# Moving a softmax scale from VectorE to ScalarE, four subtractions from TensorE to VectorE, and two places in the order

## The chip, the cores and the metric

One core of a Trainium2 chip runs the whole program. The metric is the device time of one execution in microseconds (us), the median of several runs. TensorE (PE) multiplies matrices, VectorE (DVE) and ScalarE (ACT) work elementwise, SyncE (SP) issues every DMA. Each engine works through its own queue in the written order and waits on semaphores.

## The reference

Eight batches of eight heads: x is 512 x 64 per head, state 32 x 64. A cross attention in both directions, then two feed-forward layers over the 4608 rows of 512 features that come out.

```python
scores = scale * np.matmul(x, state.transpose(0, 1, 3, 2))     # then softmax over the 32 states
xread = np.matmul(a, state)
scores2 = scale * np.matmul(state, x.transpose(0, 1, 3, 2))    # then softmax over the 512 rows
a2 /= a2.sum(-1, keepdims=True) + 1e-09
sread = np.matmul(a2, x)
attn_out = np.concatenate([xread, sread], axis=2)
h = x @ w_in;  r = np.maximum(h, 0.0);  g = s * (r * r) + b;  x = g @ w_out      # first layer
h = np.maximum(x @ w_in2, 0.0);  out = h * h @ w_out2                            # second layer
```

## The kernel before

Products are made in two fp32r parts (hi and lo): a tensor is copied to its hi part, and its lo part is the difference. A product is then three matmuls, hi by hi, hi by lo, lo by hi.

**The first layer** fills the span to about 620 us. Its rows are never formed for the reads of x: state times w_in is formed instead (the tensor S, one part per batch b and quarter q of the 2048 hidden features, in two halves r, so the tile S43 is batch 4's quarter 3, and S430 and S431 are its two PSUM tiles), and `mm1` multiplies S by the transposed attention weights aT. The list `order` says which block (j, f) of batch j and hidden feature block f is worked on in each step. A step is six matmuls of `mm1` into a tile h, three passes of ScalarE over it (`relu2`: Relu, Square, the copy to g's hi part), VectorE's `low` (g's lo part), and twelve matmuls of `mm2`, two steps later, into four accumulators acc. In blocks of the first two batches the raw weights are also converted on the way (`early`).

**Around the steps**, side jobs are put at fixed steps with `at_step(step, job, rank)`; within a step they run by rank. For batch b from 2 on, counted from its own base (base is 16 steps on from one batch to the next), step 5 makes the scores and S of quarter 0, steps 6 to 10 the softmax (`att_max`, `att_exp`, `att_sum`, `att_mul`), step 13 the transposed weights, and step 17 these, in this order: `att_sr` (rank 0: 32 calls that read x with the transposed weights, into the PSUM tile sr), `s_mm` of quarter 2 (rank 1: matmuls into two PSUM tiles, two copies on ScalarE to S's hi part), `att_scale` (rank 2: sr times the inverse of the softmax's sum s2, into srs), and `s_mm` of quarter 3 (rank 2.5). Ahead of these, in the same step, `mm2` closes the accumulators of batch b-1, and `evac` takes them out: two tiles by VectorE, two by ScalarE, each stored at once; the next `mm2` comes behind S of quarter 3.

**PSUM tiles** for all of these come from `pst`, which goes round four banks:

```python
    banks = itertools.cycle((psa, psb, psc, psc))
    def pst(name, pool=None):
        return (pool or next(banks)).tile([P, 512], F32, tag="ps", name=name)
```

A tile waits until the last reader of the tile that held its bank is done. At step 17 five tiles are taken in a row: sr, two for quarter 2, two for quarter 3.

**For batch 0**, S is made in pairs of blocks (`s_pair`), and `s_pair_lo`, one step later, makes the lo part: a matmul with minus the identity adds minus hi to the PSUM tile, and ScalarE copies the rest out.

**Lines** that the rows below name: L613 `mm1`, L643 `mm2`, L626 `low`, L350 `per_head` (the scores and S), L361 and L367 S's hi copies and lo subtractions, L560 `att_sr`, L579 and L581 the scale on ScalarE and on VectorE, L418 the matmul with minus the identity, L547 the copy of the transposed weights, L660 and L669 `evac`, L176 the last step of a conversion, L286 a job's hi copy.

**The table SUMS_AT** gives, for each of 16 jobs that prepare the second layer's weights, the steps of its 15 parts: two times (magnitude, clamp, bits), the sums, four hi copies on ScalarE, four lo subtractions on VectorE. A job's part e is stored one step after its lo subtraction. Its raw tiles and hi tiles come from one pool of four (`rawp`).

**The second layer** follows, from about 620 us to the end: a product of seven partial products per block, whose weights are loaded from DRAM.

Of the kernel before, what the change touches and what calls it, by code (L numbers as in the profile page):

```python
# [27 lines left out]
F32 = mybir.dt.float32  # L28
F32R = mybir.dt.float32r
U32 = mybir.dt.uint32  # L30
ACTF = mybir.ActivationFunctionType
ALU = mybir.AluOpType
# [16 lines left out]
VA = 4  # L49

CUTS = (0, 4, 10, NF)
# [37 lines left out]
def attn_mlp2(ctx: ExitStack, tc: tile.TileContext, xT, xn, st, w_in1, w_out1, w_in2, w_out2, s_in, b_in, out):  # L89
    nc = tc.nc  # L90
    scale = 1.0 / float(D) ** 0.5
# [8 lines left out]
    op = ctx.enter_context(tc.tile_pool(name="op", bufs=4))  # L100
# [11 lines left out]
    minus = const.tile([P, P], F32R, name="minus")  # L112
# [18 lines left out]
    def x8(shape, name, dt=F32R):  # L131
        return xp.tile(shape, dt, tag="x", name=name)
# [222 lines left out]
    def s_mm(b, q):  # L355

        t = S_t[b, q] = w8([P, 2, 2, 512], f"S{b}{q}")
        pts = [pst(f"S{b}{q}{r}") for r in range(2)]
        per_head(pts, sb_t[b], lambda rows, k: V1[q][rows, k, :])
        for r, pt in enumerate(pts):  # L360
            nc.scalar.activation(out=t[:, 0, r, :], in_=pt, func=ACTF.Copy)  # L361
            S_ps[b, q, r] = pt

    def s_rest(b, q):
        t = S_t[b, q]
        for r in range(2):
            nc.vector.tensor_tensor(  # L367
                out=t[:, 1, r, :], in0=S_ps.pop((b, q, r)), in1=t[:, 0, r, :].bitcast(F32), op=ALU.subtract
            )
# [44 lines left out]
    def s_pair_lo(f):  # L414
        q, fo = f // FQ, f % FQ * P
        t, cols = S_t[0, q], slice(fo, fo + 2 * P)
        for r, pt in enumerate(S_ps.pop(f)):
            nc.tensor.matmul(  # L418
                out=pt, lhsT=minus, rhs=t[:, 0, r, cols], start=False, stop=True, skip_group_check=True
            )  # L420
            nc.scalar.activation(out=t[:, 1, r, cols], in_=pt, func=ACTF.Copy)

    def s_lo(b, q, c):
        t, pt = S_t[b, q], S_ps.pop((b, q, c))
# [9 lines left out]
    def st_load(b):  # L434
        sb = sm.tile([P, 2, KD, NS], F32, tag="st", name=f"st{b}")
        nc.sync.dma_start(out=sb, in_=st[b])
        sb_t[b] = sb

    def att_load(b):
        t = x8([P, KD, S], f"xT{b}", F32)  # L440
        kk = KD // 2 if b < 2 else KD
        for k in range(0, KD, kk):
            nc.sync.dma_start(
                out=t[:, k : k + kk, :], in_=xT[b, k * P : (k + kk) * P].rearrange("(k p) s -> p k s", p=P)
            )
        xa[b] = [t, None]

    def att_load_n(b):
        n = x8([P, S // P, DM], f"xn{b}", F32)
        nc.sync.dma_start(out=n, in_=xn[b].rearrange("(t p) d -> p t d", p=P))  # L450
        xa[b][1] = n
# [39 lines left out]
    def att_exp(b, between=None):  # L491
        t1 = cur[b][1]
        m1 = an1.tile([P, 32, 1], F32, tag="m1", name="m1")
        nc.vector.tensor_reduce(out=m1[:, :, 0], in_=t1, axis=AX.X, op=ALU.max)
        if between:
            between()
        nc.vector.tensor_tensor(out=t1, in0=t1, in1=m1.to_broadcast([P, 32, 32]), op=ALU.subtract)
        nc.scalar.activation(out=t1, in_=t1, func=ACTF.Exp, scale=1.0 if b else scale)

    parts2 = {}  # L500

    def inverse(s, between=None):
        nc.vector.tensor_scalar(out=s, in0=s, scalar1=1e-9, scalar2=None, op0=ALU.add)
        if between:
            between()
        nc.vector.reciprocal(out=s, in_=s)
# [24 lines left out]
    def att_turn(b, c):  # L531
        turned[b, c] = att_an(b, c)
# [36 lines left out]
    def att_scale(b):  # L569
        srp = srp_t.pop(b)  # L570
        s2 = parts2.pop(b)
        if b > 1:
            inverse(s2)
        t = an1.tile([P, P], F32, tag="an", name="srs").rearrange("p (r d) -> p r d", r=2)
        srp_t[b] = t
        for r in range(2):
            src, by = srp[:, r * D : (r + 1) * D], s2[:, r : r + 1]
            if b < 2:
                nc.scalar.activation(out=t[:, r], in_=src, func=ACTF.Copy, scale=by)  # L579
            else:  # L580
                nc.vector.tensor_scalar(out=t[:, r], in0=src, scalar1=by, scalar2=None, op0=ALU.mult)  # L581

    def att_put(b):
        t = srp_t.pop(b)
        pt = pst(f"st{b}")[:, :P]
        nc.tensor.transpose(out=pt, in_=t.rearrange("p r d -> p (r d)"), identity=ident)
        dst, src = sraw[:, :, b * NS : (b + 1) * NS], pt.rearrange("p (k n) -> p k n", k=KD)
        nc.scalar.activation(out=dst, in_=src, func=ACTF.Copy)
# [547 lines left out]
    def at_step(i, fn, rank=5):  # L1136

        side.setdefault(i, []).append((rank, len(side.get(i, ())), fn))
# [5 lines left out]
    def step(j, f):  # L1144
        return place[j, 0] + f
# [4 lines left out]
    for b in range(1, B):  # L1150
        base = step(2, 0) + (b - 3) * NF if b > 1 else 0
        if b > 1:
            at_step(base + 1 + (b == 2), lambda b=b: st_load(b), 6)
            at_step(base + 1, lambda b=b: att_load(b), 6)
            at_step(base + 1, lambda b=b: att_load_n(b), 6)
            for fn, k, r in calm:
                at_step(base + k, lambda fn=fn, b=b: fn(b), r)
            for c in range(2):
                n = base + 11 + c
                at_step(n, lambda b=b, c=c: att_turn(b, c), 3)  # L1160
                at_step(n, lambda b=b, c=c: turned.pop((b, c))(), 6)
            at_step(base + (21 if b < B - 1 else 18), lambda b=b: att_put(b), -1)
            for q, (k, r) in enumerate(((5, 1), (13, 1), (17, 1), (17, 2.5))):
                at_step(base + k, lambda b=b, q=q: s_mm(b, q), r)
            at_step(base + 5 + (b == 2), lambda b=b: s_rest(b, 0), 0.2 if b == 2 else 9.8)
            at_step(base + 13, lambda b=b: s_rest(b, 1), 9.8)
            behind[base + 17] = lambda b=b: s_rest(b, 2)
            at_step(base + 18, lambda b=b: s_rest(b, 3), 0.2)
            continue
        for q, n in ((1, 12), (2, 16), (3, 23)):  # L1170
            at_step(n, lambda b=b, q=q: s_mm(b, q), 1)
            at_step(n + 1, lambda b=b, q=q: s_rest(b, q), 0.2)
# [70 lines left out]
    for f, i in zip(range(VA, NF, 2), (6, 8, 10, 15, 17, 18)):  # L1243
        at_step(i, lambda f=f: s_pair(f), 0.5)
        pre[i + 1] = [lambda f=f: s_pair_lo(f)]
# [40 lines left out]
    with tc.manual_schedule():  # L1286
# [33 lines left out]
        lo = [att_an(0, c) for c in range(2)]  # L1320
# [68 lines left out]
        lo = [att_an(1, c) for c in range(2)]  # L1389
# [14 lines left out]
        begin(4)  # L1404
        o1(3)["lo"]()
        att_scale(1)
        convert(4)
        bring(6)
# [73 lines left out]
```

## Time and profile before

| | us |
|---|---|
| median of 3 runs (1322.65 to 1323.81) | 1323.28 |
| the profiled execution's own time | 1323.02 |
| its span, first to last instruction | 1321.2 |
| TensorE busy in the span | 1304.6 (99%) |
| VectorE busy | 921.9 (70%) |
| ScalarE busy | 807.1 (61%) |

The busy times are from the head of the profile. Matmuls are pipelined and their ends are modelled, so a busy TensorE is not one without waits: a matmul's start is the safer mark. In the rows below L12 is line 12 of the kernel before; names are the program's tiles without their numbers. The granted clock is a share of TensorE's 2.4 GHz.

### The profile page before, as it was taken

Reading aid. Unit: us, or ns where it says so; the run is one execution under the profiler, and the core shown is the slowest. Engines: PE = TensorE matmul, PEld = TensorE weight load, DVE = VectorE, ACT = ScalarE, POOL = GpSimd, SP = SyncE. Lnnn points to the kernel's source line nnn. Section 1 sums busy time; section 2 is a strip of 40 time slices with the busy share of each in tenths; the row PEclk is TensorE's granted clock in tenths of the full one; section 3 lists DMA queues with packets and bytes.
Section 4 is the critical chain, followed back from the end, with each engine's and each line's share of the span. In section 5 each row is a group of like instructions: output and inputs, shape, how many; then the busy total and the mean of one; then the engine's idle time right before and its main releaser. Section 6 shows DMA issues by size and latency. Waiting matters only on the chain.

```text
span 1321.2 us, 21087 instructions
## 1 busy us (share of the span) xinstructions
PE 1304.6 (99%) x7434; PEld 1115.6 (84%) x7434; DVE 921.9 (70%) x1609; ACT 807.1 (61%) x1485; POOL 0.7 (0%) x7
## 2 busy tenths in 40 slices
PE   6999999999999999999999999999999999999998
PEld 4677777778787877788988888888899999999998
DVE  7988988766676767655556668656775776678665
ACT  5877657676666667665744565545555565565554
POOL 0000000000000000000000000000000000000000
PEclk8999999999999999999999999999999999999999
DMA  8367443453725254451465577665887798788775
GB/s 280 129 215 258 153 145 109 144 183 105 255 92 204 88 180 157 131 171 38 160 199 174 176 247 219 207 173 171 258 259 230 227 323 255 227 265 298 246 223 167
DMA packets 159560, 255.68 MB, mean 194 GB/s; under 512 B 14816, under 2 KB 67040, under 8 KB 159200
## 3 DMA queue, kind: packets, MB, share of 16 engines
q1 hardware_dynamic: 159456, 254.34, 60.2%
q8 instruction: 60, 0.98, 0.3%
q14 instruction: 44, 0.36, 0.1%
HBM read 202.90 MB, written 51.38 MB: 192 GB/s over the span
## 4 chain that ended last, share of the span: by engine, by line
PE 95%; DVE 3%; ACT 1%; DMA 0%; issue 0%; DVEq 0%
PE acc L643 27%; PE p L899 25%; PE m L875 25%; PE h L613 15%; PE S L350 2%; PE sr L560 1%; PE sc L350 1%; PE tp L546 0%; DMA i1r<-w_in 0%; DVE sraw L316 0%; DVE g L626 0%; DVE V L169 0%; DVE part L660 0%; DVE v L169 0%; DVE V L176 0%
## 5 line engine op out<-in xcount | busy, mean ns | idle before, releaser
L875 PE MATMUL m<-bigx,bigr 128*128 128x384 f32 (+1 forms) x1680 | 366.9, 356 | 0.0
L643 PE MATMUL acc<-g,o1h 128*128 128x512 f32 (+1 forms) x1152 | 340.8, 378 | 1.1 <-DVE g L626 0.8
L875 PEld LDWEIGHTS m<-bigx,bigr 128*128 128x128 f32 x1680 | 302.6, 188 | 26.5
L643 PEld LDWEIGHTS acc<-g,o1h 128*128 128x128 f32 x1152 | 211.4, 188 | 46.6 <-issue 4.2
L643 PE MATMUL acc<-g,o1l 128*128 128x512 f32 (+1 forms) x576 | 217.4, 377 | 0.0
L613 PE MATMUL h<-aT,S 128*128 128x512 f32 x768 | 197.5, 394 | 0.0
L626 DVE TENSOR_TENSOR g<-r,g 128x512 fp32r<-128x512 f32 (+1 forms) x144 | 94.7, 657 | 141.2 <-ACT g L622 141.2
L899 PE MATMUL p<-g,bigr 128*128 128x384 f32 (+1 forms) x864 | 191.1, 356 | 0.0
L613 PEld LDWEIGHTS h<-aT,S 128*128 128x128 f32 x768 | 142.7, 188 | 45.9 <-ACT a2T L547 5.0
L899 PEld LDWEIGHTS p<-g,bigr 128*128 128x128 f32 x864 | 155.9, 188 | 13.1
L620 ACT ACTIVATE r<-h 128x512 f32<-128x512 f32 (+1 forms) x144 | 82.2, 571 | 111.7 <-PE h L613 109.1
L702 ACT ACTIVATE sc<-sc 128x384 f32<-128x384 f32 (+1 forms) x120 | 68.0, 567 | 101.3 <-DVE sc L705 100.0
L899 PE MATMUL p<-bigg,bigr 128*128 128x384 f32 (+1 forms) x576 | 129.7, 357 | 0.0
L643 PEld LDWEIGHTS acc<-g,o1l 128*128 128x128 f32 x576 | 108.4, 188 | 20.3
L899 PEld LDWEIGHTS p<-bigg,bigr 128*128 128x128 f32 x576 | 104.0, 188 | 9.0
L702 ACT ACTIVATE v<-m 128x384 f32<-128x384 f32 (+1 forms) x80 | 42.8, 535 | 94.7 <-PE m L875 94.2
L705 DVE TENSOR_TENSOR v<-m,r 128x384 f32<-128x384 f32 (+1 forms) x40 | 24.5, 612 | 106.6 <-PE m L875 106.6
L621 ACT ACTIVATE r<-r 128x512 f32<-128x512 f32 (+1 forms) x144 | 87.9, 610 | 4.6
L622 ACT ACTIVATE g<-r 128x512 fp32r<-128x512 f32 (+1 forms) x144 | 87.8, 610 | 4.6
L705 DVE TENSOR_TENSOR g<-bigt,g 128x384 fp32r<-128x384 f32 (+1 forms) x71 | 41.9, 604 | 16.4 <-ACT g L702 16.3
L705 DVE TENSOR_TENSOR r<-m,v 128x384 f32<-128x384 f32 (+1 forms) x40 | 24.5, 612 | 34.6 <-PE m L875 31.9
L702 ACT ACTIVATE t<-t 128x384 f32<-128x384 f32 (+1 forms) x80 | 45.2, 565 | 1.3
(156 smaller groups left out, 1544.9 us busy)
## 6 DMA issues: line engine op xcount, KB each, us to landing
bigr<-wi SPq DMA_DIRECT2D x280, 256.0 KB, 3.2
bigr<-wo SPq DMA_DIRECT2D x240, 256.0 KB, 3.3
i1r<-w_in SPq DMA_DIRECT2D x16, 512.0 KB, 4.3
o1r<-w_out SPq DMA_DIRECT2D x16, 512.0 KB, 5.1
xn<-xn SPq DMA_DIRECT2D x8, 1024.0 KB, 9.3
x<-ot SPq DMA_DIRECT2D x32, 256.0 KB, 2.6
i2r<-w_in SPq DMA_DIRECT2D x32, 256.0 KB, 4.1
o2r<-w_out SPq DMA_DIRECT2D x16, 512.0 KB, 4.2
```

The costliest lines, as they stand in the source:

```text
L350: nc.tensor.matmul(out=outs[r][k * NS : (k + 1) * NS], lhsT=state[rows, r, k, :], rhs=moving(rows, k), start=True, stop=True, skip_group_c ...
L560: nc.tensor.matmul(out=srp[k * NS : (k + 1) * NS, r * D : (r + 1) * D], lhsT=a2Ts[r][:, i, k * NS : (k + 1) * NS], rhs=n[:, i, h * D : (h ...
L613: nc.tensor.matmul(out=hp, lhsT=l_, rhs=r_, start=(i == 0), stop=(i == len(ops) - 1))
L620: nc.scalar.activation(out=r, in_=hp, func=ACTF.Relu)
L621: nc.scalar.activation(out=r, in_=r, func=ACTF.Square)
L622: nc.scalar.activation(out=g[:, 0], in_=r, func=ACTF.Copy)
L626: nc.vector.tensor_tensor(out=g[:, 1], in0=r, in1=g[:, 0].bitcast(F32), op=ALU.subtract)
L643: nc.tensor.matmul(out=o, lhsT=l_, rhs=r_, start=(opens and i == 0), stop=(closes and i == 2))
L702: nc.scalar.activation(out=c, in_=src, func=func)
L705: nc.vector.tensor_tensor(out=out, in0=x, in1=y, op=op)
L875: nc.tensor.matmul(out=o, lhsT=w[:, a, k, :], rhs=x[:, b, k, :], start=(start and k + a + b == 0), stop=(k + a == 2), skip_group_check=True,)
L899: nc.tensor.matmul(out=o, lhsT=w[:, a], rhs=g[:, b], start=(opens and e == 0), stop=(u == NU - 1 and e == 2), skip_group_check=True,)
```

## The change

- `s_pair_lo`: for four of the six pairs (first blocks 6, 8, 12 and 14) VectorE subtracts hi from the PSUM tile; the two matmuls with minus the identity and ScalarE's two copies fall away. Pairs 4 and 10 stay.
- `att_scale`: for batches 2 to 7 ScalarE scales sr, as it did for batches 0 and 1, in place of VectorE. The sums' inverse (two small VectorE operations) moves from step 17 to step 8, behind `att_exp`.
- `att_load_n`: for batches 3 to 7 the load of xn (x by rows, for `att_sr`) is issued at step 4 in place of step 1.
- SUMS_AT, tenth row: the second hi copy goes from step 84 to 85, which is batch 6's step 5, its lo subtraction from 85 to 86, its store with it.

```diff
@@ -68,7 +68,7 @@
     (64, 64, 66, 66, 66, 67, 67, 68, 68, 68, 68, 69, 69, 69, 70),
     (70, 71, 71, 71, 71, 74, 75, 76, 75, 76, 76, 77, 76, 77, 77),
     (75, 76, 78, 78, 78, 78, 79, 80, 79, 80, 80, 81, 80, 82, 82),
-    (82, 82, 82, 82, 83, 83, 84, 86, 84, 87, 87, 87, 85, 88, 89),
+    (82, 82, 82, 82, 83, 83, 84, 86, 85, 87, 87, 87, 86, 88, 89),
     (87, 87, 87, 87, 90, 91, 92, 94, 92, 94, 94, 95, 93, 95, 95),
     (92, 93, 94, 95, 95, 96, 98, 99, 98, 99, 99, 100, 99, 100, 100),
     (98, 98, 99, 100, 100, 101, 103, 104, 102, 105, 105, 106, 104, 106, 107),
@@ -415,10 +415,12 @@
         q, fo = f // FQ, f % FQ * P
         t, cols = S_t[0, q], slice(fo, fo + 2 * P)
         for r, pt in enumerate(S_ps.pop(f)):
-            nc.tensor.matmul(
-                out=pt, lhsT=minus, rhs=t[:, 0, r, cols], start=False, stop=True, skip_group_check=True
-            )
-            nc.scalar.activation(out=t[:, 1, r, cols], in_=pt, func=ACTF.Copy)
+            hi, lo = t[:, 0, r, cols], t[:, 1, r, cols]
+            if f not in (VA, CUTS[2]):
+                nc.vector.tensor_tensor(out=lo, in0=pt, in1=hi.bitcast(F32), op=ALU.subtract)
+                continue
+            nc.tensor.matmul(out=pt, lhsT=minus, rhs=hi, start=False, stop=True, skip_group_check=True)
+            nc.scalar.activation(out=lo, in_=pt, func=ACTF.Copy)
 
     def s_lo(b, q, c):
         t, pt = S_t[b, q], S_ps.pop((b, q, c))
@@ -496,6 +498,8 @@
             between()
         nc.vector.tensor_tensor(out=t1, in0=t1, in1=m1.to_broadcast([P, 32, 32]), op=ALU.subtract)
         nc.scalar.activation(out=t1, in_=t1, func=ACTF.Exp, scale=1.0 if b else scale)
+        if b > 1:
+            inverse(parts2[b])
 
     parts2 = {}
 
@@ -569,16 +573,11 @@
     def att_scale(b):
         srp = srp_t.pop(b)
         s2 = parts2.pop(b)
-        if b > 1:
-            inverse(s2)
         t = an1.tile([P, P], F32, tag="an", name="srs").rearrange("p (r d) -> p r d", r=2)
         srp_t[b] = t
         for r in range(2):
             src, by = srp[:, r * D : (r + 1) * D], s2[:, r : r + 1]
-            if b < 2:
-                nc.scalar.activation(out=t[:, r], in_=src, func=ACTF.Copy, scale=by)
-            else:
-                nc.vector.tensor_scalar(out=t[:, r], in0=src, scalar1=by, scalar2=None, op0=ALU.mult)
+            nc.scalar.activation(out=t[:, r], in_=src, func=ACTF.Copy, scale=by)
 
     def att_put(b):
         t = srp_t.pop(b)
@@ -1152,7 +1151,7 @@
         if b > 1:
             at_step(base + 1 + (b == 2), lambda b=b: st_load(b), 6)
             at_step(base + 1, lambda b=b: att_load(b), 6)
-            at_step(base + 1, lambda b=b: att_load_n(b), 6)
+            at_step(base + (4 if b > 2 else 1), lambda b=b: att_load_n(b), 6)
             for fn, k, r in calm:
                 at_step(base + k, lambda fn=fn, b=b: fn(b), r)
             for c in range(2):
```

What the change does to the order is plain from the diff but for three places.

TensorE at batch 4's step 17, with the engines that each row waits for: the last row of `att_sr` and the first two of S43. Before:

```order
L560 MATMUL sr4_3316<-xn4_2696,a2T_3147 32x64 x31
L350 MATMUL S420_3350<-V2_744,st4_2692 32x512
L350 MATMUL S421_3351<-V2_744,st4_2692 32x512 [waits Activation_49]
L350 MATMUL S430_3368<-V3_1099,st4_2692 32x512 [waits Activation_49]
L350 MATMUL S431_3369<-V3_1099,st4_2692 32x512 [waits DVE_49,PE_49]
```

Now:

```order
L564 MATMUL sr4_3310<-xn4_2789,a2T_3141 32x64 x31
L350 MATMUL S420_3344<-V2_744,st4_2684 32x512
L350 MATMUL S421_3345<-V2_744,st4_2684 32x512 [waits Activation_49]
L350 MATMUL S430_3360<-V3_1095,st4_2684 32x512 [waits Activation_49]
L350 MATMUL S431_3361<-V3_1095,st4_2684 32x512 [waits PE_49,Activation_49]
```

S431 takes the bank of sr4. The wait for VectorE in its row was for the scale; now it is for ScalarE. Batches 3, 5, 6 and 7 read alike. At batch 2, S231 now waits for VectorE still, for it has got the bank of S220 (free after VectorE's first S22 subtraction), and the next tile, h22, has sr's.

ScalarE at the same place, from the evacuation's second tile to the next Relu. Before:

```order
L667 ACTIVATE ot_3313<-acc33_2707,cs_109,s_sb_107 128x512
L361 ACTIVATE S42_3349<-S420_3350 128x512
L361 ACTIVATE S42_3349<-S421_3351 128x512
L361 ACTIVATE S43_3367<-S430_3368 128x512
L361 ACTIVATE S43_3367<-S431_3369 128x512
L620 ACTIVATE r_3418<-h42_3411 128x512
```

Now:

```order
L666 ACTIVATE ot_3307<-acc33_2697,cs_109,s_sb_107 128x512
L361 ACTIVATE S42_3343<-S420_3344 128x512
L361 ACTIVATE S42_3343<-S421_3345 128x512
L580 ACTIVATE srs_3356<-sr4_3310,s2_2896 128x64 x2
L361 ACTIVATE S43_3359<-S430_3360 128x512
L361 ACTIVATE S43_3359<-S431_3361 128x512
L619 ACTIVATE r_3408<-h42_3401 128x512
```

The scale (srs) stands behind the two copies of quarter 2 and ahead of the two of quarter 3.

ScalarE at batch 6's step 5 (o2h10 is the moved hi copy, h55 the tile of that step's `mm1`, sc60 and S600 the scores and S of quarter 0). Before:

```order
L622 ACTIVATE g_4160<-r_4159 128x512
L286 ACTIVATE o2h10_4181<-v_4115 128x512
L620 ACTIVATE r_4196<-h55_4189 128x512
L621 ACTIVATE r_4196<-r_4196 128x512
L622 ACTIVATE g_4197<-r_4196 128x512
L465 ACTIVATE sc_4226<-sc60_4216 128x512
L361 ACTIVATE S60_4229<-S601_4231 128x512
```

Now:

```order
L621 ACTIVATE g_4150<-r_4149 128x512
L619 ACTIVATE r_4187<-h55_4180 128x512
L620 ACTIVATE r_4187<-r_4187 128x512
L621 ACTIVATE g_4188<-r_4187 128x512
L467 ACTIVATE sc_4217<-sc60_4207 128x512
L361 ACTIVATE S60_4220<-S601_4222 128x512
L286 ACTIVATE o2h10_4174<-v_4105 128x512
```

The hi copy has gone from ahead of the Relu of h55 to behind the copies of S60.

## Rows read from the trace of the kernel before

**Rows 1.** Windows, 190 to 620 us: TensorE busy (matmuls), granted clock, DMA share, GB/s.

```profile
190.00:620.00 430.00, 430.00 (x2511) 1.00 0.44 146
```

**Rows 2.** Timeline, 79 to 83 us: start, length, engine, line, operation, [idle before <-releaser].

```profile
79.98 0.40 PE L418 MATMUL S<-S,minus 128*128 128x256 f32 x2
80.21 0.63 PE L643 MATMUL acc<-g,o1h 128*128 128x512 f32 x2
...
80.98 0.69 DVE L176 SCALAR_TENSOR_TENSOR v<-o1r,v 128x512 uint32<-128x512 uint32 x1
...
82.96 1.52 PE L613 MATMUL h<-aT,S 128*128 128x512 f32 x6
```

**Rows 3.** Timeline, ScalarE before batch 6's step 5.

```profile
423.15 0.63 ACT L286 ACTIVATE o2h<-v 128x512 fp32r<-128x512 f32 x1 [3.94 <-DMA wo<-o2h]
```

**Rows 4.** The chain (start, length): S at step 5 of batches 6 and 7.

```profile
425.18 1.72 PE S L350 x16
...
498.81 0.86 PE S L350 x16
```

**Rows 5.** Timeline at batch 4's step 17.

```profile
332.80 1.95 PE L350 MATMUL S<-V,st 64*32 64x512 f32 x32
332.93 0.48 DVE L581 TENSOR_SCALAR srs<-sr,s 128x64 f32<-128x64 f32 x2 [0.65 <-PE sr L560]
...
333.97 2.07 ACT L361 ACTIVATE S<-S 128x512 fp32r<-128x512 f32 x4 [0.22 <-PE S L350]
...
334.67 0.73 PE L643 MATMUL acc<-g,o1h 128*128 128x512 f32 x2
```

**Rows 6.** The chain near 40 us: the scale on ScalarE, and a copy.

```profile
39.74 0.52 ACT srs L579 x2
...
42.59 0.48 ACT a2T L547
```

**Rows 7.** Timeline, TensorE at 43 us: fourteen S matmuls after a wait.

```profile
43.12 1.09 PE L350 MATMUL S<-V,st 64*32 64x512 f32 x14 [1.01 <-ACT a2T L547]
44.13 1.10 PE L560 MATMUL sr<-xn,a2T 128*32 128x64 f32 x64
```

**Rows 8.** Timeline at batch 2's step 17.

```profile
183.57 2.72 DVE L660 SCALAR_TENSOR_TENSOR part<-acc,s_sb,part 128x512 f32<-128x512 f32 x4
...
186.27 1.08 ACT L361 ACTIVATE S<-S 128x512 fp32r<-128x512 f32 x2 [2.89 <-PE S L350]
...
187.07 0.68 DVE L626 TENSOR_TENSOR g<-r,g 128x512 fp32r<-128x512 f32 x1
...
187.30 1.09 PE L350 MATMUL S<-V,st 64*32 64x512 f32 x14 [0.31 <-DVE srs L581]
...
188.27 1.28 DVE L367 TENSOR_TENSOR S<-S,S 128x512 fp32r<-128x512 f32 x2
```

**Rows 9.** Timeline at step 17 of batch 3, and of batch 7.

```profile
260.68 0.69 ACT L669 ACTIVATE ot<-acc,s_sb 128x512 f32<-128x512 f32 x1 [2.62 <-DMA x<-ot]
261.07 0.73 PE L643 MATMUL acc<-g,o1h 128*128 128x512 f32 x2
261.27 2.05 ACT L361 ACTIVATE S<-S 128x512 fp32r<-128x512 f32 x4
...
553.13 2.07 ACT L361 ACTIVATE S<-S 128x512 fp32r<-128x512 f32 x4 [1.32 <-PE S L350]
...
553.93 0.73 PE L643 MATMUL acc<-g,o1h 128*128 128x512 f32 x2
```

**Rows 10.** The page's DMA issues: KB each, us to landing.

```profile
xn<-xn SPq DMA_DIRECT2D x8, 1024.0 KB, 9.3
```

**Rows 11.** Windows of the start: TensorE's busy time and granted clock.

```profile
15.00:18.00 3.00, 0.47 (x3) 0.50 1.02 412
21.00:24.00 3.00, 2.70 (x18) 0.50 0.89 259
...
42.00:45.00 3.00, 1.99 (x76) 1.00 0.04 14
```

## The prediction

> **What bounds the kernel now.** I read the windows first. From 190 to 620 us TensorE is busy for all of its 430 us at a granted clock of 1.00, which is the 2.4 GHz level [rows 1]; this is the stretch in which nearly all of the change lies. So the time is the sum of what stands in TensorE's queue: what leaves that queue is gained, and what makes it wait is lost, at full price, since nothing later waits that could pay it back. VectorE is busy for 70% of the span and ScalarE for 61% (the table above); work on them counts only where TensorE waits for it. So I went on to the places in the timeline where TensorE starts something that another engine lets go.
>
> Because the ends of matmuls are modelled, a busy TensorE can hide a wait. The chain shows one: the sixteen matmuls of S at batch 6's step 5 take 1.72 us, those of batch 7 0.86 [rows 4]. ScalarE explains it: at 423.15 us its hi copy had waited 3.94 us for a store, and the Relu behind it, which frees a PSUM bank, was late [rows 3].
>
> **The change, part by part.** All sums are against the profiled execution, 1323.02 us; the median of the runs lies 0.26 us above it.
>
> *Matmuls with minus the identity.* Two of them stand between 79.98 us and the next matmul at 80.21 [rows 2]: 0.23 us a pair, four pairs, so **-0.92 us**. Their work goes to VectorE, eight subtractions of 128x256. No row shows one from PSUM at this size; two of 128x512 take 1.28 us [rows 8], so 0.64 us each bounds it from above, and nothing bounds it from below. What hides it: at the pair that ends at 80.2 us VectorE's conversions end at 80.98 + 0.69 = 81.67 [rows 2]; the first subtraction ends by 82.31, the second by 82.95. The block that reads them starts at 82.96 - 0.23 = 82.73, its third matmul (the first to read a lo part) 0.23 x 2 later, at 83.19, its sixth at 83.88. That leaves 0.9 us. If this cover went, each microsecond of VectorE's would be TensorE's. The cost is nothing; ScalarE's eight copies that go were hidden too.
>
> *The moved hi copy.* It now stands behind the copies of S60, so the Relu of h55 no longer waits for a store. S at step 5 goes from 1.72 to the 0.86 of the other batches: **-0.86 us** [rows 4]. Its lo subtraction and its store, one step later, are read by nothing before the second layer.
>
> *The load of xn.* Three steps later for five batches. It lands 9.3 us after its issue [rows 10] and is read at step 17, thirteen steps of six and twelve matmuls after step 4; at 0.23 us a matmul [rows 2] that is some 54 us. On SP's queue the raw weights behind it are issued earlier, which nobody waits for. Cost: nothing.
>
> *The inverse at step 8.* Two small VectorE operations, far ahead of their reader: nothing.
>
> *The scale on ScalarE.* Here I expect the loss. S431, the second tile of quarter 3, takes sr's bank and cannot start before the scale has read it. Before, VectorE scaled at 332.93 and was done at 333.41, while TensorE was still in quarter 2 [rows 5]: no wait. Now the scale stands on ScalarE behind two copies that themselves wait for quarter 2's last matmul. So TensorE must finish quarter 2, let ScalarE copy twice and scale twice, and only then go on. In batch 4 the copies begin at 333.97 [rows 5]; two take 1.08 us [rows 8], two scales 0.52 us [rows 6], 1.60 together, so the bank is free at 335.57. TensorE goes on 0.05 us behind ScalarE: the copy that starts at 42.59 ends 0.48 later, at 43.07 [rows 6], and S goes on at 43.12, with the same fourteen matmuls left, which take 1.01 us until the next group at 44.13 [rows 7]. So `mm2` starts at 335.57 + 0.05 + 1.01 = 336.63 where it started at 334.67 [rows 5]: +1.96 us. By the same working, from the start of the copies to that of `mm2`:
> - batch 7: 553.13 + 1.60 + 1.06 = 555.79 against 553.93 [rows 9]: +1.86. Batches 5 and 6 repeat batch 4's rows: +1.96 each.
> - batch 3: ScalarE's copies start at 261.27 only, for its evacuation at 260.68 had waited 2.62 us for a store, while `mm2` started at 261.07 [rows 9], before they were done. Now TensorE has to wait for that too: 261.27 + 1.60 + 1.06 = 263.93, **+2.86**.
> - batch 2: S231 waits for VectorE's first subtraction of S22. VectorE is free of the partial sums at 183.57 + 2.72 = 186.29; the g part and a weight sum take 1.20 us from 187.07 to 188.27, the subtraction 0.64 [rows 8]; it ends at 188.13, and TensorE goes on at 188.18 where it went on at 187.30 [rows 8]: +0.88.
>
> Together 0.88 + 2.86 + 3 x 1.96 + 1.86 = **+11.48 us**.
>
> The bounds of this term: the least is two copies and two scales (1.60 us) less the 0.1 us of TensorE's own start, for five batches, with batch 2's 0.88: 8.4 us. The most adds to the sum a slower scale on ScalarE, at the 0.64 us of a 128x512 operation in place of 0.26, twice in five batches: 11.48 + 3.8 = 15.3 us. I take 11.48, for rows 6 and 7 show the same operations in the same order of events.
>
> **The sum:** -0.92 - 0.86 + 11.48 = +9.70 us on 1323.02, 1332.7; with the 0.26 us to the median **1333.0 us**, slower by 0.73%. A measurement of this kernel can tell about 0.2% (2.6 us) from no change.
>
> **The rivals.**
>
> *The clock falls in the waits.* TensorE now stands still five times for about 2 us and more. At the start its clock goes to 0.50, the 1.2 GHz level, in a stretch where it was busy for 0.47 of 3 us, and stays there from 21 to 24 us though busy for 2.70 [rows 11]. Against it: a wait of much the same shape, before the S matmuls at 43.12, left the clock at 1.00 with 1.99 of 3 us busy [rows 11]. Batch 3's wait is the longest and so the likeliest. A fall costs half of the work done until it rises: with 2.70 us of such work in the row, 1.4 us for that row, some 2 us with the rest. That gives 1335 us for batch 3 alone and 1343 for five batches.
>
> The Trainium skill ("TensorE: Matmul & The Clock Gate", section "A second HAM failure mode: psum-queue depth-cycling") speaks against this change: where the matmuls go round PSUM banks and pause between groups, the gate may close again and again. By that rule the time would be this rival's upper one. The trace does not bear it out so far, by the row at 42 to 45 us.
>
> *Not slower: the bank is free in time.* If ScalarE were through with the scale before TensorE has issued quarter 2 and S430, no wait would come in, and batch 2's present one (TensorE idle 0.31 us and more before 187.30 [rows 8]) would go as well. That one is worth at most 187.30 - 186.27 = 1.03 us, from the end of S22's matmuls, where ScalarE's copies start, to TensorE's going on [rows 8]. Then only gains are left: 0.92 + 0.86 + 1.03 = 2.81 us off the median, 1320.5 us, 0.2% faster. It decides at `mm2`'s old start less 1.06: in batch 4 the scale would have to end by 333.61, before the first copy begins at 333.97. For it speaks only that VectorE managed this; the order on ScalarE speaks against it.
>
> *Half of it comes back.* VectorE and ScalarE go on while TensorE waits, and a wait hidden later in the modelled ends would shrink: half of 11.48 is 5.74 us less, 1327.3 us. Apart from the one at batch 6 I find no such wait; the steps all repeat alike.
>
> *The change does not do what it says:* its instructions are seen in the order, and all are where they should be.
>
> **How the numbers follow.** The forecast has 0.79, the clock 0.08, the free bank 0.06, the half 0.07. The range is the forecast's own: from the lower bound (8.4 - 1.8 = 6.6 us, 1329.9 with the median's offset) to the sum with a scale that costs half of its bound's excess and one fall of the clock, 1333.0 + 1.9 + 2, about 1336.9. Chances: slower 0.92 (forecast, clock, half); faster 0.03 and same 0.05, from the free bank, which lies at the border, and a rest for a bank assignment that I read wrongly.
>
> **What would show it.** In the trace after: the matmuls with minus the identity twelve down to four; S at batch 6's step 5 at 0.86 us; S at step 17 no longer as one group of 32 but as eighteen and fourteen, the fourteen released by ScalarE's scale, with TensorE idle before them in batches 3 to 7, longest in batch 3, and by VectorE in batch 2; the granted clock 1.00 throughout. The windows from 190 to 620 us then show some 10 us of TensorE idle or hidden, and the second layer starts as much later. I am wrong if the thirty-two still run through, if VectorE's subtractions hold up a block of batch 0, or if the clock falls.

## The result, and the profile after

| | before | changed |
|---|---|---|
| median, us | 1323.43 (6 runs, 1322.65 to 1324.13) | 1335.14 (6 runs, 1333.26 to 1337.35) |
| the profiled execution's own time | 1323.02 | 1337.35 |
| its span | 1321.2 | 1334.3 |
| TensorE busy in the span | 1304.6 | 1312.0 |

The ratio is 1.0089, with a 95% interval of 1.0077 to 1.0100: slower by 11.7 us. The time lies within the forecast's range, 2.1 us above its centre. The profiled execution happens to be the longest of the six.

First the window of [rows 1] again: 5.8 of the 430 us are now idle, and the rest of the loss is hidden in modelled ends.

```profile
190.00:620.00 430.00, 424.16 (x2447) 331.03 (x2446) 276.87 (x479) 281.62 (x501) 0.00 (x0) 1.00 0.44 146
```

Two lines' summaries of the changed kernel (ns of one: least, median, most; first and last start in us). The matmuls with minus the identity are down from twelve to four, and VectorE has its eight subtractions, at 0.41 us each:

```profile
L422 PE MATMUL S<-S,minus x4: 278/280/281, 62.5 to 103.4; 128*128 128x256 f32 x4
L420 DVE TENSOR_TENSOR S<-S,S x8: 411/414/417, 71.6 to 119.1; 128x256 fp32r<-128x256 f32 x8
```

The timeline of the changed kernel at step 17 of batches 2, 3, 4 and 7 (start, length, engine, line, operation, [idle before <-releaser]):

```profile
185.31 1.90 PE L350 MATMUL S<-V,st 64*32 64x512 f32 x18
...
187.46 0.52 ACT L580 ACTIVATE srs<-sr,s 128x64 f32<-128x64 f32 x2
187.93 1.28 DVE L367 TENSOR_TENSOR S<-S,S 128x512 fp32r<-128x512 f32 x2
188.67 1.09 PE L350 MATMUL S<-V,st 64*32 64x512 f32 x14 [1.47 <-DVE S L367]
189.69 0.50 PE L642 MATMUL acc<-g,o1h 128*128 128x512 f32 x1
...
262.06 0.69 ACT L668 ACTIVATE ot<-acc,s_sb 128x512 f32<-128x512 f32 x1 [2.62 <-DMA x<-ot]
262.65 1.07 ACT L361 ACTIVATE S<-S 128x512 fp32r<-128x512 f32 x2
...
263.60 0.53 ACT L580 ACTIVATE srs<-sr,s 128x64 f32<-128x64 f32 x2
264.18 1.09 PE L350 MATMUL S<-V,st 64*32 64x512 f32 x14 [1.71 <-ACT srs L580]
265.20 0.74 PE L642 MATMUL acc<-g,o1h 128*128 128x512 f32 x2
...
336.96 1.90 PE L350 MATMUL S<-V,st 64*32 64x512 f32 x18
338.31 0.78 ACT L666 ACTIVATE ot<-acc,cs,s_sb 128x512 f32<-128x512 f32 x1 [2.39 <-DMA x<-ot]
338.99 1.07 ACT L361 ACTIVATE S<-S 128x512 fp32r<-128x512 f32 x2
...
339.94 0.53 ACT L580 ACTIVATE srs<-sr,s 128x64 f32<-128x64 f32 x2
340.52 1.09 PE L350 MATMUL S<-V,st 64*32 64x512 f32 x14 [1.66 <-ACT srs L580]
341.54 1.22 PE L642 MATMUL acc<-g,o1h 128*128 128x512 f32 x2
...
563.31 1.90 PE L350 MATMUL S<-V,st 64*32 64x512 f32 x18
...
565.46 0.52 ACT L580 ACTIVATE srs<-sr,s 128x64 f32<-128x64 f32 x2
566.03 1.09 PE L350 MATMUL S<-V,st 64*32 64x512 f32 x14 [0.82 <-ACT srs L580]
567.05 0.73 PE L642 MATMUL acc<-g,o1h 128*128 128x512 f32 x2
```

The group of 32 [rows 5] has split into 18 and 14. Ahead of the 14 stands the order on ScalarE: evacuation, two copies, scale; TensorE goes on 0.05 us behind the scale (565.46 + 0.52 = 565.98, then 566.03). In batch 2 VectorE's subtraction releases it. From the start of S to the start of `mm2`, in us, each the difference of two starts in the timeline:

| batch | before | changed | loss | forecast |
|---|---|---|---|---|
| 2 | 3.22 | 4.38 | 1.16 | 0.88 |
| 3 | 1.88 | 4.62 | 2.74 | 2.86 |
| 4 | 1.87 | 4.58 | 2.71 | 1.96 |
| 5 | 1.87 | 3.74 | 1.87 | 1.96 |
| 6 | 1.87 | 3.75 | 1.88 | 1.96 |
| 7 | 1.98 | 3.74 | 1.76 | 1.86 |

These are 12.12 us where 11.48 were forecast. Batch 4 stands out: its second evacuation waited for a store and started 2.38 us behind `sr`. In the kernel before it started 1.22 us behind `sr` (at 331.76):

```profile
332.98 0.78 ACT L667 ACTIVATE ot<-acc,cs,s_sb 128x512 f32<-128x512 f32 x1 [1.23 <-PE sr L560]
```

And behind this wait the clock fell, as windows of the changed kernel show (length, TensorE busy, loads, VectorE, ScalarE, POOL, granted clock, DMA share, GB/s):

```profile
340.00:342.00 2.00, 1.48 (x15) 0.64 (x16) 0.90 (x2) 0.78 (x4) 0.00 (x0) 0.89 0.75 193
342.00:344.00 2.00, 2.00 (x6) 1.54 (x6) 1.29 (x2) 0.77 (x2) 0.00 (x0) 0.50 0.88 261
344.00:346.00 2.00, 2.00 (x9) 1.60 (x8) 0.00 (x0) 0.00 (x0) 0.00 (x0) 0.76 0.86 264
```

The ledger of the profiled execution, from the starts of `sr`: between batch 4's and batch 5's lie 77.08 us in place of 72.76, 4.32 more; 2.71 is the wait, so the fall cost 1.61. Between batch 0's and batch 2's lie 144.68 in place of 145.49: the pairs, -0.81. Between batch 5's and 6's 74.64 in place of 73.64: less batch 5's 1.87, that is -0.87 at batch 6's step 5. `sr` of batch 0 starts at 39.59 in place of 38.57; over the twelve traces of this case it lies between 38.42 and 39.75, by and large the later the longer the clock stays at 0.50 at the start (from 26 to 27 us it is 0.50 here and 1.00 in the kernel before), so this +1.02 is taken as scatter of the start. Together 12.12 + 1.61 - 0.81 - 0.87 + 1.02 = 13.07 us, of the 13.1 us between the spans.

### The profile page after: what moved, and what is told of

Read it like the earlier page. It is cut to its first block, busy times and chain, and to the rows that moved or that the text cites. A ratio compares the mean times of both kernels' runs of the same rounds, so it can differ in the third digit from the quotient of the medians.

```text
span 1334.3 us, 21070 instructions
## 1 busy us (share of the span) xinstructions
PE 1312.0 (98%) x7426; PEld 1118.2 (84%) x7426; DVE 921.5 (69%) x1605; ACT 806.3 (60%) x1489; POOL 0.7 (0%) x7
## 4 chain that ended last, share of the span: by engine, by line
PE 92%; DVE 4%; ACT 2%; DMA 1%; issue 1%; SPq 0%; POOLq 0%; POOL 0%; DVEq 0%; ACTq 0%
PE acc L642 25%; PE p L898 25%; PE m L874 25%; PE h L612 14%; PE S L350 2%; DMA o1r<-w_out 1%; DVE sraw L316 1%; PE sc L350 1%; DVE g L625 1%; PE on L1283 1%; DMA x<-ot 0%; PE tp L550 0%; ACT S L361 0%; PE sr L564 0%; DVE V L169 0%
## 5 line engine op out<-in xcount | busy, mean ns | idle before, releaser
L898 PEld LDWEIGHTS p<-g,bigr 128*128 128x128 f32 x864 | 155.9, 188 | 13.1
L367 DVE TENSOR_TENSOR S<-S,S 128x512 fp32r<-128x512 f32 x54 | 34.7, 684 | 29.4 <-ACT S L361 29.4
L704 DVE TENSOR_TENSOR g<-bigt,g 128x384 fp32r<-128x384 f32 (+1 forms) x71 | 41.8, 602 | 16.5 <-ACT g L701 16.3
L350 PE MATMUL S<-V,st 64*32 64x512 f32 (+1 forms) x544 | 40.2, 561 | 8.9 <-ACT srs L580 5.8
```

What stands on the lines that cost most here:

```text
L350: nc.tensor.matmul(out=outs[r][k * NS : (k + 1) * NS], lhsT=state[rows, r, k, :], rhs=moving(rows, k), start=True, stop=True, skip_group_c ...
L367: nc.vector.tensor_tensor(out=t[:, 1, r, :], in0=S_ps.pop((b, q, r)), in1=t[:, 0, r, :].bitcast(F32), op=ALU.subtract)
L704: nc.vector.tensor_tensor(out=out, in0=x, in1=y, op=op)
L898: nc.tensor.matmul(out=o, lhsT=w[:, a], rhs=g[:, b], start=(opens and e == 0), stop=(u == NU - 1 and e == 2), skip_group_check=True,)
```

## The experiments

All edits are to the changed kernel, unless it says otherwise.

### The scale back on VectorE

```diff
         for r in range(2):
             src, by = srp[:, r * D : (r + 1) * D], s2[:, r : r + 1]
-            nc.scalar.activation(out=t[:, r], in_=src, func=ACTF.Copy, scale=by)
+            if b < 2:
+                nc.scalar.activation(out=t[:, r], in_=src, func=ACTF.Copy, scale=by)
+            else:
+                nc.vector.tensor_scalar(out=t[:, r], in0=src, scalar1=by, scalar2=None, op0=ALU.mult)
```

> The changed kernel with one part undone: for batches 2 to 7 VectorE scales sr again (the inverse stays at step 8; the pairs, the hi copy and the xn load stay moved). My theory, that the scale's place behind ScalarE's two copies makes the whole loss: what is left is -0.92 us (pairs) and -0.86 us (hi copy), so 1323.4 - 1.8 = 1321.6 us, S at step 17 again one group of 32 in batches 3 to 7, S at batch 6's step 5 at 0.86 us, clock 1.00 throughout 190 to 620 us. Rival, that another part costs (VectorE's subtractions for four pairs, or xn's later load among the stores): the time stays above 1326 us and a wait stands in batch 0's blocks or before sr. Rival, that the gains are hidden: 1323.4 us, no change.

Measured: 1321.52 us against 1323.40, ratio 0.9982 (0.9973 to 0.9991). The timeline at batch 4's step 17:

```profile
331.18 1.95 PE L350 MATMUL S<-V,st 64*32 64x512 f32 x32
331.31 0.47 DVE L583 TENSOR_SCALAR srs<-sr,s 128x64 f32<-128x64 f32 x2 [0.93 <-PE sr L564]
...
332.69 0.78 ACT L669 ACTIVATE ot<-acc,cs,s_sb 128x512 f32<-128x512 f32 x1 [2.56 <-DMA x<-ot]
333.05 0.73 PE L645 MATMUL acc<-g,o1h 128*128 128x512 f32 x2
```

The 32 run through in 1.87 us. The scale is the whole loss, and the other parts together gain 1.9 us. The inverse's new place has a part in this: at batch 2, S starts at 183.94 us and `mm2` at 186.69, 2.75 us in place of 3.22, since VectorE goes from the partial sums straight to the scale; in the kernel before, the inverse stood between them. The store is late here too (2.56 us of waiting), and costs nothing: `mm2` starts before the copies do. Only the scale's new place lets TensorE feel it.

### The scale alone, in the kernel before

```diff
-        if b > 1:
-            inverse(s2)
...
-            if b < 2:
-                nc.scalar.activation(out=t[:, r], in_=src, func=ACTF.Copy, scale=by)
-            else:
-                nc.vector.tensor_scalar(out=t[:, r], in0=src, scalar1=by, scalar2=None, op0=ALU.mult)
+            nc.scalar.activation(out=t[:, r], in_=src, func=ACTF.Copy, scale=by)
```

with the inverse behind `att_exp`, as in the change.

> The kernel before with one part of the change alone: ScalarE scales all batches' reads, with the inverse at step 8. My theory by the forecast's term: 1323.4 + 11.5 = 1334.9 us. By the changed kernel's own profile the loss of this part is larger, since batch 4's evacuation waited for a late store (+0.8 us) and the clock fell behind its wait (+1.7 us): 1335.14 + 1.78 - 1323.4 = 13.5 us, so 1336.9 us. If xn's moved load makes batch 4's store late, this kernel, where it is not moved, has batch 4's wait at 0.8 us like batches 5 to 7 and no fall of the clock, and comes out at 1334.5 to 1335. Rival, that the loss comes from the parts together: under 1330 us.

Measured: 1335.27 us (1334.66 to 1335.45), ratio 1.0086 (1.0073 to 1.0100). Batch 4's wait is 0.83 us here. But the clock fell all the same, this time behind batch 3's wait of 1.70 us, which in the changed kernel's own profile (1.71 us) had left it at 1.00:

```profile
264.00:266.00 2.00, 1.67 (x16) 0.74 (x17) 0.70 (x2) 0.79 (x4) 0.00 (x0) 0.88 0.81 183
266.00:268.00 2.00, 2.00 (x7) 1.51 (x6) 1.29 (x2) 0.58 (x2) 0.00 (x0) 0.50 0.92 260
```

The second reading is at batch 6's step 5, where the hi copy has not been moved. The timeline's row of the copy, and the chain's row of S:

```profile
431.37 0.63 ACT L286 ACTIVATE o2h<-v 128x512 fp32r<-128x512 f32 x1 [2.48 <-DMA wo<-o2h]
```

```profile
434.85 0.86 PE S L350 x16
```

The copy has waited 2.48 us for the store in place of 3.94 [rows 3], and S takes 0.86 us, not 1.72 [rows 4]. From batch 5's `sr` to batch 6's it is 74.67 us, as in the changed kernel (74.64). So with the waits at step 17 this loss goes by itself; that was tried directly below.

### sr in another bank

```diff
-        srp = srp_t[b] = pst(f"sr{b}")
+        if b < 2:
+            srp = pst(f"sr{b}")
+        else:
+            next(banks)
+            srp = pa.tile([P, 512], F32, tag="acc", name=f"sr{b}")
+        srp_t[b] = srp
```

> The changed kernel, scale on ScalarE behind the two copies as it is, but for batches 2 to 7 sr takes a PSUM bank of the accumulators' pool instead of one of the four that go round (that one is passed over, so the rest of the round stays). Then S431 takes a bank that has long been free, and the scale's bank is needed only by the fourth accumulator, some 2 us after the first product of mm2. My theory (the wait is for sr's bank): the waits of step 17 go, 1321.6 us within 1.5 us, S as one group of 32. Rival, that the later copies on ScalarE themselves hold TensorE up (the scale delays quarter 3's copies and the Relu): most of the loss stays, 1330 us or more, with the waits before mm1 or mm2 instead. Rival, that the wait moves to the fourth accumulator: up to 1 us a batch, 1323 to 1327 us.

Measured: 1321.16 us, ratio 0.9982 (0.9974 to 0.9991). Batch 4's step 17 in the timeline:

```profile
330.68 1.95 PE L350 MATMUL S<-V,st 64*32 64x512 f32 x32
...
332.56 0.73 PE L647 MATMUL acc<-g,o1h 128*128 128x512 f32 x2
332.86 0.53 ACT L585 ACTIVATE srs<-sr,s 128x64 f32<-128x64 f32 x2
```

The scale stands where the change has put it, behind the two copies, and even starts after `mm2`. Nobody waits for it in this trace, since S431 does not take its bank. So ScalarE's load is not the cause, and its order costs time only through the bank that the scale holds. The price of the new bank is small: batch 2's `sr` now waits 0.24 us for VectorE to read the accumulator.

### The scale ahead of the copies

```diff
-            (att_sr, 17, 0), (att_scale, 17, 2))
+            (att_sr, 17, 0), (att_scale, 17, 0.5))
```

> The changed kernel with the scale still on ScalarE, but put ahead of quarter 2's copies in step 17. My theory: S431 then waits only for the second evacuation and the scale. Worked from the kernel before's rows: batch 4 evacuation ends 333.76, scale 0.52, start 0.05: 334.33 against 333.61, +0.7; batch 3 261.37 + 0.57 = 261.94 against 260.01, +1.9; batches 5 and 6 some 1.0 and 0.9; batch 7 and 2 nothing, and batch 2's old wait partly goes (-0.5). Sum +4.0 with -1.8 of the gains: 1325.7 us, within 2 us; the waits before the last 14 matmuls of S shrink by the 1.08 us of two copies. Rival, that the place on ScalarE does not matter and the engine's load does: about 1335 us.

Measured: 1325.68 us, ratio 1.0015 (1.0006 to 1.0024). Batch 4 in the timeline:

```profile
333.87 0.78 ACT L666 ACTIVATE ot<-acc,cs,s_sb 128x512 f32<-128x512 f32 x1 [2.20 <-PE S L350]
334.55 0.51 ACT L580 ACTIVATE srs<-sr,s 128x64 f32<-128x64 f32 x2
...
335.11 1.09 PE L350 MATMUL S<-V,st 64*32 64x512 f32 x14 [0.49 <-ACT srs L580]
336.12 0.74 PE L642 MATMUL acc<-g,o1h 128*128 128x512 f32 x2
```

What is left of the wait is the evacuation and the scale. From S to `mm2` it is 3.64 us in batch 3, 3.41 in 4, 2.80 in 5, 2.59 in 6, 1.87 in 7 and 1.88 in 2. Where the second evacuation waits for nothing (7) or is VectorE's (2), there is no loss. That the time meets the 1325.7 us of the expectation is in part luck: against the kernel before the six places make +3.5 us in place of +4.0, with batch 4 at +1.54 in place of +0.7 (a late store again) and batch 2 at -1.34 in place of -0.5.

### The scale done twice, and four times

```diff
-            nc.scalar.activation(out=t[:, r], in_=src, func=ACTF.Copy, scale=by)
+            for _ in range(2 if b > 1 else 1):
+                nc.scalar.activation(out=t[:, r], in_=src, func=ACTF.Copy, scale=by)
```

> The changed kernel with the scale of batches 2 to 7 done twice on ScalarE (0.52 us more behind the two copies). My theory: each of the five waits of batches 3 to 7 grows by 0.52 us, batch 2's not (its S231 waits for VectorE): +2.6 us, 1337.7 us, with waits of 2.2 us in batches 3 and 4 and 1.35 in 5 to 7. Rival, that half of a wait is hidden again later: 1336.4 us. Clock: if a longer wait is what lets it fall, both of the long waits (3 and 4) now fall in the same run, 1.6 us more: 1339.3 us; if it is chance at any length, falls appear also behind batches 5 to 7.

> The changed kernel with the scale of batches 2 to 7 done four times on ScalarE (1.56 us more). My theory without the clock: 5 x 1.56 = +7.8 us, 1342.9 us, waits of 2.4 us in batches 5 to 7 and 3.2 in 3 and 4. If the clock falls behind each wait of more than about 1.7 us, as it did once behind one of 1.66 us here and once behind one of 1.70 us with the scale alone, all five fall at 1.6 us each, one of which the changed kernel has already: 1342.9 + 6.4 = 1349.3 us. If it falls behind some only, in between.

Measured: 1340.28 us, ratio 1.0129 (1.0115 to 1.0143), and 1352.19, ratio 1.0220 (1.0206 to 1.0234). Batch 5's wait in the timeline and the windows behind it, first with two scales, then with four:

```profile
418.76 1.09 PE L350 MATMUL S<-V,st 64*32 64x512 f32 x14 [1.52 <-ACT srs L581]
```

```profile
420.00:422.00 2.00, 2.00 (x10) 1.60 (x10) 1.29 (x2) 1.01 (x2) 0.00 (x0) 1.00 0.80 182
```

```profile
424.04 1.57 PE L350 MATMUL S<-V,st 64*32 64x512 f32 x14 [2.90 <-ACT srs L581]
```

```profile
424.00:426.00 2.00, 1.96 (x15) 0.63 (x16) 0.00 (x0) 0.35 (x1) 0.00 (x0) 0.63 0.83 138
426.00:428.00 2.00, 2.00 (x6) 1.52 (x6) 1.29 (x2) 0.73 (x2) 0.00 (x0) 0.52 0.87 266
```

A second pair of scales costs 0.70 us, not 0.52 (four take 1.22 where two took 0.52): two that write different halves of the tile start 0.20 us apart, two that write the same half 0.35. The wait grows by exactly this, from 0.82 to 1.52 us in batch 5. Five times 0.70 are 3.5 us; the clock fell behind both long waits (2.38 and 1.89 us), one fall more than in the changed kernel's profile, 1.6 us. Together these are the 5.1 us between the medians, though how often the clock fell in the runs without a trace is not known.

With four scales (2.60 us, so 5 x 2.08 = 10.4 us more) the clock fell behind all five waits (2.90 to 3.77 us). From `sr` to `sr`, less what the waits add, the falls behind batches 4 to 6 cost 1.6 us each. The one behind batch 3, whose wait was the longest, cost 2.8 us: TensorE went on at 264.93 us, and four to six us later the clock was still at 0.51:

```profile
268.94:270.94 2.00, 2.00 (x6) 1.52 (x6) 0.00 (x0) 0.00 (x0) 0.00 (x0) 0.51 1.10 388
```

The spans of the two profiled executions lie 16.3 us apart: 10.0 us of longer waits (batch 4's was long in the changed kernel already), 7.6 us of falls (2.8 and four of 1.6, less the one there), and 1.3 us less at the start, the pairs and batch 2. So nothing of a wait comes back, and a longer wait costs the fall on top.

### The load of xn back at step 1

```diff
-            at_step(base + (4 if b > 2 else 1), lambda b=b: att_load_n(b), 6)
+            at_step(base + 1, lambda b=b: att_load_n(b), 6)
```

> The changed kernel with xn's load for batches 3 to 7 back at step 1. In the five traces so far, batch 4's first store landed, counted from the start of sr, 1.2 us later where xn's load is not moved (the kernel before and the scale alone) and 1.6 to 2.6 us later where it is. Theory that the moved load (through what then stands on the DMA queues) makes this store late: the second evacuation of batch 4 starts 1.2 us behind sr again, TensorE's wait there is 0.8 us instead of 1.66, and the time falls by 0.85 us, by up to 2.5 us with the clock's fall: 1332.7 to 1334.3 us, with less spread between runs. Rival, that the store's landing scatters by itself: 1.6 us or later here too, and 1335.1 us as before.

Measured: 1333.82 us (1332.75 to 1335.21), ratio 1.0080 (1.0068 to 1.0093), a spread that overlaps the changed kernel's. The time lies in the theory's range, but the theory's sign is not there: batch 4's second evacuation starts 1.94 us behind `sr` where the theory had 1.2, TensorE's wait is 1.22 us where it had 0.8, and the clock stays at 1.00:

```profile
338.98 1.09 PE L350 MATMUL S<-V,st 64*32 64x512 f32 x14 [1.22 <-ACT srs L580]
```

In the run with six pairs, below, where the load is moved, the evacuation starts at 1.21. So the moved load is not needed for a late store, nor does it always bring one. Over the three traces with the load at step 1 the start lies at 1.21 to 1.94 us, over the nine others at 1.21 to 3.08: that the move makes late stores more frequent is not excluded. The cause of the late store stays open.

### The hi copy back

```diff
-    (82, 82, 82, 82, 83, 83, 84, 86, 85, 87, 87, 87, 86, 88, 89),
+    (82, 82, 82, 82, 83, 83, 84, 86, 84, 87, 87, 87, 85, 88, 89),
```

> The changed kernel with the hi copy back at step 84. The forecast's step (the move alone takes 0.86 us off) gives 1335.1 + 0.86 = 1336.0 us, with S at batch 6's step 5 at 1.72 us again. The rival, from the trace of the scale alone: TensorE's waits at step 17 have already moved step 5 away from the store that the copy waits for, so S stays at 0.86 us wherever the copy stands, and the distance from batch 5's sr to batch 6's stays at 74.6 us: 1335.1 us, no change from the changed kernel.

Measured: 1333.67 us (1332.96 to 1334.90), ratio 1.0078 (1.0066 to 1.0091). The copy's row in the timeline and S's in the chain:

```profile
427.68 0.63 ACT L286 ACTIVATE o2h<-v 128x512 fp32r<-128x512 f32 x1 [1.37 <-DVE v L176]
```

```profile
432.28 0.86 PE S L350 x16
```

The copy waits for no store at all, S takes 0.86 us, and from batch 5's `sr` to batch 6's it is 74.64 us. The time does not rise; that it came out lower is not more than the two kernels' runs scatter (in this profile, too, no clock fell). The rival holds: beside the scale's waits no worth of the move is seen.

### All six pairs on VectorE

```diff
-            if f not in (VA, CUTS[2]):
+            if f >= 0:
```

on top of `sr` in another bank.

> The changed kernel with sr in an accumulators' bank (as in the run with sr in another bank, 1321.16 us) and with VectorE's subtraction for all six pairs of batch 0 instead of four. My theory: two pairs more at 0.23 us each, 1321.16 - 0.46 = 1320.7 us, 0.2% under the kernel before, no matmul with minus the identity left. Rival, that VectorE has no room at the first of the two (block 4, where the first conversions still run): a wait before mm1 there, 1321.5 us or more.

Measured: 1321.48 us, ratio 0.9986 (0.9977 to 0.9995): no gain over four pairs. At the pair that the change leaves alone, the timeline shows the rival:

```profile
65.99 0.76 DVE L420 TENSOR_TENSOR S<-S,S 128x256 fp32r<-128x256 f32 x2
66.47 1.20 PE L617 MATMUL h<-aT,S 128*128 128x512 f32 x4 [0.46 <-DVE S L420]
```

VectorE's conversions end at 66 us only, the block's third matmul waits. At the other left pair, from 102.40 us to the block behind it, it takes 6.02 us where it took 5.58 with the matmuls. From batch 0's `sr` to batch 2's lie 145.74 us, where four pairs and the same bank took 144.82: in the trace the two pairs more cost 0.92 us.

### The bank from batch 3 on

`sr` in an accumulators' bank for batches 3 to 7; batch 2 keeps the round, with its scale ahead of the copies:

```diff
-        if b < 2:
+        if b < 3:
             srp = pst(f"sr{b}")
...
-                at_step(base + k, lambda fn=fn, b=b: fn(b), r)
+                at_step(base + k, lambda fn=fn, b=b: fn(b), 0.5 if fn is att_scale and b == 2 else r)
```

> The changed kernel with sr in an accumulators' bank for batches 3 to 7 only; for batch 2 sr stays in the round and its scale stands ahead of the two copies (as in the run with the scale before the copies, where batch 2 had no wait). In the run with all six in the accumulators' pool, batch 2's sr itself waited 0.24 us for VectorE to read the accumulator. Expected: that wait gone, no wait at any step 17, 1321.16 - 0.3 = 1320.9 us, 0.19% under the kernel before. Rival, that batch 2's scale ahead of the copies delays quarter 2: 1321.2 us or more.

Measured: 1320.80 us, ratio 0.9981 (0.9972 to 0.9990), the fastest version here; that it beats the two at 1321.2 and 1321.5 is not shown, the intervals overlap. Batch 2 in the timeline, without the wait that the kernel before had [rows 8]:

```profile
184.73 1.95 PE L350 MATMUL S<-V,st 64*32 64x512 f32 x32
184.87 0.52 ACT L585 ACTIVATE srs<-sr,s 128x64 f32<-128x64 f32 x2 [1.85 <-PE sr L569]
...
186.61 0.73 PE L647 MATMUL acc<-g,o1h 128*128 128x512 f32 x2
```

But one wait is left at a step 17, the one that the expectation of the run with `sr` in another bank had as a rival, at the fourth accumulator. Batch 4's store was the latest of all traces here (its evacuation started 3.08 us behind `sr`), the scale came late with it, and the weights of the fourth accumulator's first matmul, which takes the bank that the scale reads, waited for it:

```profile
334.77 0.53 ACT L585 ACTIVATE srs<-sr,s 128x64 f32<-128x64 f32 x2
335.35 0.30 PEld L647 LDWEIGHTS acc<-g,o1h 128*128 128x128 f32 x2 [0.48 <-ACT srs L585]
```

From batch 4's `sr` to batch 5's it is 73.11 us in place of 72.76, a loss of 0.35 us. In the other two traces with `sr` in an accumulators' bank it is 72.76 us.

## Why the prediction was right, and where it was not

**The mechanism and its price held.** S431 takes `sr`'s bank, so TensorE waits for whatever ScalarE does ahead of the scale: with the scale on VectorE, or `sr` in another bank, the loss is gone; with the scale further ahead on ScalarE it shrinks to 3.5 us, where 4.0 were worked out from rows of the kernel before. The terms of batches 3, 5, 6 and 7 came out 0.08 to 0.12 us under the forecast, batch 2's at 0.85 to 0.95 us in five other traces and 1.16 in the profiled one; the six places together carry 12.1 of the 13.1 us.

**Batch 4's term was mis-sized**, 1.96 us forecast, 2.71 measured. It took the evacuation's start from one trace, where the store had landed early. I had seen that batch 3's evacuation waits for a store, and not asked how much such a landing scatters in the batches where it happened to be hidden: 1.2 to 3.1 us behind `sr`, over twelve traces of batch 4.

**The clock's fall was a rival with 8 in 100, and it happened.** Falls and late stores, some 2 us together, are as large as what separates the median from the forecast's centre, and the runs of the changed kernel spread over 4 us where 27 of the kernel before spread over 2.5. The forecast's argument against it, the start-up wait of 1.01 us [rows 7] that left the clock alone [rows 11], was true for a wait of that size and said nothing of 1.7 us. The rival's own size held: 2 us were estimated for a fall, 1.6 measured. But it is not an alternative to the waits; it comes on top of the longest. The profiled executions without a fall, of the kernels with xn's load or the hi copy back, took 1333.04 and 1332.96 us, which is the forecast. The mean granted clock, which is on record for each run, agrees: of the sixteen runs of these two kernels and the changed one, the eight at a mean of 0.996 took 1332.75 to 1333.82 us, the eight at 0.994 or 0.995 took 1333.81 to 1337.35. But a longer stretch at 0.50 at the start lowers this mean too (0.995 in the profiled run with six pairs, where no clock fell later), so which runs had a fall behind a wait is not shown. Of "TensorE: Matmul & The Clock Gate", section "A second HAM failure mode: psum-queue depth-cycling", in the Trainium skill: its rule that pauses between groups on cycling PSUM banks close the gate is borne out for the long pauses of this kernel, not for those of 0.8 us, which never did it. The rival's upper time of 1343 us, with a fall behind all five waits, did not come.

**The hi copy** does what the forecast said, -0.87 us at its place, and so with the scale back on VectorE (72.76 us from `sr` to `sr`, in place of 73.64). The step that fails is that I added it to the scale's term as if each stood alone, and gave back nothing: "Apart from the one at batch 6 I find no such wait" names the very wait that the scale's delay takes away by itself. Without the move the changed kernel is not slower. That the sum came out all the same is luck: this 0.87 us comes off either way, once, by the move or by the scale's delay.

**The pairs** were worth 0.81 us in the profiled execution and 0.98 to 1.01 in seven other traces with the same four pairs and `sr` in the round, for 0.92 forecast. The subtraction takes 0.41 us where the bound was 0.64. For that price "VectorE: DVE Perf Modes" in the Trainium skill, section "The TRN2 errata — SBUF-src ops pay a fixed extra latency per instruction", gives for an fp32 add of two tensors (N + 151)/0.96 ns, 424 ns at 256 columns, an estimate; the trace's 414 ns, with one operand in PSUM, agrees within 3%. That the cover is thin was seen at six pairs: at the two that the change leaves out it is not there.

**xn's load and the inverse** cost nothing that could be told, and the inverse's place gained 0.47 us at batch 2 where VectorE scales; the forecast had it at nothing. Whether the load has a part in batch 4's late store is open.

## What to carry to other kernels

Before work is moved to an engine that is less busy, look at which buffer it frees, who takes that buffer next, and what stands ahead of it in the new engine's queue: here 0.5 us of scaling cost some 12 us over six batches, because a bank then hung on two copies behind a matmul, and in batches 3 and 4 on an evacuation that hangs on a store. If the new place is wanted, give the buffer another bank, which made the same order free but for 0.35 us behind the latest store. A wait that is hidden in one trace still scatters; before another one is put behind it, ask what its late case costs. And gains found one by one in a profile are not added to a loss that shifts the same waits.

## What the runs showed of the hardware

The clock behind TensorE's waits at step 17, from windows of 2 us in seven traces: at 1.00 behind every wait of 0.49 to 1.52 us (26 of them); of five waits of 1.66 to 1.71 us, two were followed by a clock at 0.50 and three were not; behind all seven of 1.89 to 3.77 us it fell. It was back at 1.00 within 6 us of TensorE's going on. A fall cost 1.6 us, the one behind the longest wait 2.8. Two waits of nearly the same length in one execution (1.71 and 1.66 us, batches 3 and 4 of the changed kernel) so differed by 1.6 us. These waits are the idle time that the profile shows; at batches 5 and 6 of the changed kernel it shows 0.82 us where 1.87 and 1.88 us were lost.

The evacuation behind batch 4's first store of 256 KB started 1.2 to 3.1 us behind `sr` in nearly the same program, the one at batch 3 at 2.50 to 2.52 us in all twelve traces.

Two scales on ScalarE, each into its half of a tile, took 0.52 us together; four that write each half twice took 1.22, since two into the same half started 0.35 us apart in place of 0.20.
